# A fused cross-attention and squared-ReLU feed-forward on one core: loads, transposes and PSUM banks rearranged

## The chip, the core and the metric

The kernel runs on one core of a Trainium2 chip. A core has a matrix engine (TensorE, PE in the profile, with its weight loads as PEld), VectorE (DVE), ScalarE (ACT), GpSimd (POOL), SyncE (SP), which here only issues transfers, and 16 DMA engines that all queues share. The metric is device time in microseconds, smaller is better.

## What is computed

```python
# x: (B=8, H=8, S=512, D=64); state: (8, 8, Ns=32, 64)
scores = scale * x @ state.T              # per batch and head, softmax over the 32 slots
xread  = softmax(scores, -1) @ state      # 512 rows read the state
scores2 = scale * state @ x.T             # softmax over the 512 rows
sread  = softmax(scores2, -1) @ x         # 32 slots read x
a = concatenate([xread, sread], axis=2)   # (8, 8, 544, 64) -> 4352 rows of 512
h = a @ w_in                              # 512 -> 2048
g = s * relu(h)**2 + b
out = g @ w_out                           # 2048 -> 512, float32
```

## The kernel before, in words

Matrix operands are float16, sums float32. Heads are handled in two groups g of four; a group's four times 32 slots fill the 128 partitions. For each batch b:

- `att_stT` (L186) transposes the batch's state on TensorE; `att_xT` (L199), called twice, does so with x in eight 128x128 matmul transposes each, and DVE copies them out of PSUM.
- `att_T` (L216): scores T, 16 matmuls of 64x32 weights, into two one-bank tiles; ScalarE takes exponentials E (L235) with the row sums rs.
- `att_D` (L244), once per group: a matmul with a block matrix of ones sums E over the slots; logarithm L (L249), exponential R of its negative (L251), and a4 = E * R on DVE are the softmax weights.
- `att_M` (L256): the product of the state with w_in, M, in four chunks c of 512 columns, so that mm1 can multiply a4 straight with M (xread @ w_in without xread). Eight matmuls per chunk, into two one-bank tiles.
- `att_aT` (L278): E divided by its row sums on DVE (a2), eight TensorE transposes and a DVE copy make aT; `att_V` (L293) multiplies x (as weights) with 32 columns of aT, 32 matmuls, and writes the slot reads, already transposed, into srdT for all batches.
- `mm1_f` (L331), for each of 16 chunks f of 128 hidden columns: two matmuls of 512 columns into h, ReLU on ScalarE (r, L340; for a third of batch 0's chunks on DVE, L338), square on DVE (g, L342). In the trace h, r and g have f in their names.
- `mm2_part` (L347): the output tile o of 128 rows (rr, four per batch) sums 16 matmuls of 512 columns, in four parts of four (here called units); DVE scales and adds the bias (osb, L361), and SP stores it (L362).

TensorE's order is written out by hand. Of 16 slots per batch, each gives one mm1 chunk, then the pieces of the attention of the next batch (the lists in `pieces` and `first`), then one unit of mm2, which lags 20 slots behind mm1. After batch 7 come 16 slots of mm1 for the 256 slot reads (`mm1_sr`, h_sr), mixed with the last units, and two output tiles of slot reads. `bias` sums w_out with 16 matmuls and one more product in the mm2 of batch 0. `warm_up` issues matmuls on zeros before the first real ones. The tile framework orders the other engines by their priorities and adds the waits.

Loads: SP brings x of batch 0 as float32 in four pieces (xf, L92), which DVE and ScalarE cast (L116). Pool loads and casts in one DMA each: four chunks of w_in (wi, L144), x of batches 1 to 7 (xn, L134), four chunks of w_out (wo, L154), and twice the state of batches 2 to 7 (L169), side by side, as the transposes need it. The state of batches 0 and 1 comes as float32 (stf), and Pool casts batch 0's (L123).

PSUM has 8 banks: three buffers of one bank for the attention (psA), three for h (psH), two for o (psO).

Of the kernel before, what the change touches and what calls it, by code (L numbers as in the profile page):

```python
# [14 lines left out]
def kernel(  # L15
# [10 lines left out]

    nc = tc.nc
    AF = mybir.ActivationFunctionType  # L30
    ALU = mybir.AluOpType

# [7 lines left out]
    NG = H // 4  # L40
    NPAIR = H // 2
# [3 lines left out]
    NFC = DF // FC  # L45
    scale = float(1.0 / np.sqrt(D))
# [7 lines left out]
    mpool = ctx.enter_context(tc.tile_pool(name="mpool", bufs=2))  # L54
# [3 lines left out]
    psA = ctx.enter_context(tc.tile_pool(name="psA", bufs=3, space=bass.MemoryType.PSUM))  # L58
    psH = ctx.enter_context(tc.tile_pool(name="psH", bufs=3, space=bass.MemoryType.PSUM))
# [25 lines left out]
    st_v = state.rearrange("b (g hf) j d -> (hf j) (b g) d", g=NG)
    stf = konst.tile([P, 2 * NG, D], FP32, name="stf")
    xf = konst.tile([P, H, SCH * D], FP32, name="xf")
    x0_v = x[0].rearrange("h (q c) d -> q h (c d)", q=P)
    nc.scalar.dma_start(stf[:, 0:NG, :], st_v[:, 0:NG, :])
    nc.scalar.dma_start(ident16, ident_dr.ap())  # L90
    for i in range(4):
        nc.sync.dma_start(xf[:, 2 * i : 2 * i + 2], x0_v[:, 2 * i : 2 * i + 2])  # L92
    nc.scalar.preload_act_table_set("natural_log_exp_and_others")
# [12 lines left out]
    srdT = konst.tile([P, NPAIR, B * Ns], FP16, name="srdT")

    st16 = konst.tile([P, B * NG, 2, D], FP16, name="st16")
    xn = {}
    xn[0] = xpool.tile([P, H, SCH, D], FP16, name="xn_0")

    def cast_x0(eng, i):
        eng(  # L116
            xn[0][:, 2 * i : 2 * i + 2].rearrange("p h c d -> p h (c d)"),
            xf[:, 2 * i : 2 * i + 2],
        )

    def cast_st(eng, b):
        for k in range(2):
            eng.tensor_copy(st16[:, b * NG : b * NG + NG, k, :], stf[:, b * NG : b * NG + NG])  # L123

    cast_st(nc.gpsimd, 0)
    cast_x0(nc.vector.tensor_copy, 0)
    cast_x0(nc.scalar.copy, 1)
    cast_x0(nc.vector.tensor_copy, 2)
    cast_x0(nc.scalar.copy, 3)
    cast_st(nc.vector, 1)  # L130

    def load_x(b):
        xt = xpool.tile([P, H, SCH, D], FP16, name=f"xn_{b}")
        nc.gpsimd.dma_start(  # L134
            out=xt.rearrange("p h c d -> p h (c d)"),
            in_=x[b].rearrange("h (q c) d -> q h (c d)", q=P),
        )
        xn[b] = xt

    wi = []  # L140

    def load_wi(c):
        t = wpool.tile([P, NKM, FC], FP16, name=f"wi_{c}")
        nc.gpsimd.dma_start(  # L144
            out=t,
            in_=moe_w_in.rearrange("(k p) f -> p k f", p=P)[:, :, c * FC : (c + 1) * FC],
        )
# [12 lines left out]
    load_wi(0)  # L160
    load_wi(1)
    load_x(1)
    load_wi(2)
    load_wi(3)
    for q in range(4):
        load_wo(q)
    load_x(2)
    for k in range(2):
        nc.gpsimd.dma_start(out=st16[:, 2 * NG :, k, :], in_=st_v[:, 2 * NG :, :])  # L169
    for b in range(3, B):  # L170
        load_x(b)
# [4 lines left out]
    def head_of(g, q):  # L176
        return 4 * g + (q if g == 0 else q ^ 1)

    def chunk_of(cc):

        return 2 * (cc % 2) + cc // 2


    A = {}

    def att_stT(b):  # L186
        ps = att_ps([P, NG, P], FP16, f"stTps_{b}")
        for g in range(NG):
# [10 lines left out]
    def att_xT(b, i):  # L199
# [10 lines left out]
        if b == 0 and i == 1:  # L210
            nc.scalar.copy(xT, ps)
        else:
            nc.vector.tensor_copy(xT, ps)
# [291 lines left out]
```

## Time and profile before

| | us |
|---|---|
| median of the three runs (257.17 to 259.74) | 257.67 |
| span of the profiled execution, first to last instruction | 256.8 |
| TensorE busy | 235.6 |
| DVE busy | 146.6 |
| ScalarE busy | 118.1 |
| last matmul ends | 249.1 |

The profiled execution's own time is not listed apart from its span; the median lies 0.9 us above the span. Times in a timeline or a chain are counted from the span's start. A row of the timeline gives start, duration, engine, line, operation, output <- inputs, shapes, and in brackets how long the engine had been idle and what ended that.

### The profile page before, as it was taken

To read this page: it belongs to the slowest core of one execution; us is meant where nothing else is said; L and a number is where in the kernel's file an instruction comes from. 1 tells how busy PE (TensorE), PEld (TensorE's weight loads), DVE (VectorE), ACT (ScalarE), POOL (GpSimd) and SP (SyncE) were. 2 spreads that over 40 slices of the span, in tenths; PEclk is the share of its full clock that TensorE was granted. 3 is DMA by queue.
4 is the path that set the end of the run, shared out by engine and by line. 5 is a ranking of instruction groups with operands and counts; after the bars stand their busy time and mean duration, and the time that the engine had idled before them with its cause. 6 is when DMAs were issued, how large, how long until landed. Compare 5 with 4: busy or idle time off the path is not lost.

```text
span 256.8 us, 4444 instructions
## 1 busy us (share of the span) xinstructions
PE 235.6 (92%) x1772; PEld 108.9 (42%) x1772; DVE 146.6 (57%) x327; ACT 118.1 (46%) x255; POOL 15.0 (6%) x23
## 2 busy tenths in 40 slices
PE   8189759997999999999999999999999999999970
PEld 3034214442543454445434544454344444555430
DVE  1128968777468745874587458745874444433220
ACT  2074564862457445743574357435743444222000
POOL 6524210000000000000000000000000000000000
PEclk9679986999999999999999999999999999999998
DMA  7999999901111111111111111111101211121111
GB/s 169 198 195 207 203 181 198 139 0 41 43 41 41 43 41 43 41 41 46 41 43 41 43 41 44 40 41 43 52 31 46 79 42 41 43 82 41 50 52 65
DMA packets 21709, 18.71 MB, mean 73 GB/s; under 512 B 5048, under 2 KB 17336, under 8 KB 21688
## 3 DMA queue, kind: packets, MB, share of 16 engines
q0 software_dynamic: 14608, 8.26, 22.9%
q1 hardware_dynamic: 6664, 10.06, 11.3%
q8 instruction: 14, 0.23, 0.4%
q10 hardware_dynamic: 416, 0.10, 0.2%
q14 instruction: 7, 0.06, 0.1%
HBM read 17.76 MB, written 8.91 MB: 104 GB/s over the span
## 4 chain that ended last, share of the span: by engine, by line
PE 83%; DVE 6%; DMA 4%; ACT 2%; issue 1%; SPq 1%
DMA xf<-in_x_dram 4%; PE o_2_2011 L66 1%; PE o_3_974 L66 1%; PE o_2_2372 L66 1%; PE o_1_1921 L66 1%; PE o_2_2733 L66 1%; PE o_2_1650 L66 1%; PE o_2_1289 L66 1%; PE o_1_1199 L66 1%; PE o_0_728 L66 1%; PE o_1_2643 L66 1%; PE o_1_2282 L66 1%; PE o_1_1560 L66 1%; PE o_3_2109 L66 1%; PE o_3_1748 L66 1%; PE o_0_2554 L66 1%
## 5 line engine op out<-in xcount | busy, mean ns | idle before, releaser
L66 PE MATMUL warm_ps<-warm 128*128 128x512 f16 x26 | 9.9, 521 | 7.1 <-DVE stT_171 L196 5.2
L66 PEld LDWEIGHTS <-warm 128*128 128x128 f16 x26 | 3.0, 124 | 10.6 <-issue 9.0
L116 DVE CAST xn_115<-xf 128x512 f16<-128x512 f32 x2 | 0.9, 452 | 9.2 <-DMA xf<-in_x_dram 9.2
L116 ACT CAST xn_115<-xf 128x512 f16<-128x512 f32 x2 | 1.2, 618 | 9.5 <-DMA xf<-in_x_dram 9.5
L66 PEld LDWEIGHTS <-M_253 128*128 128x128 f16 x32 | 2.6, 103 | 6.0 <-DVE M_253 L276 3.5
L66 PEld LDWEIGHTS <-M_1502 128*128 128x128 f16 x32 | 3.1, 98 | 3.8
L66 PEld LDWEIGHTS <-M_760 128*128 128x128 f16 x32 | 3.1, 98 | 3.8
L66 PEld LDWEIGHTS <-M_1863 128*128 128x128 f16 x32 | 3.1, 98 | 3.8
L66 PEld LDWEIGHTS <-M_2224 128*128 128x128 f16 x32 | 3.1, 98 | 3.8
L66 PEld LDWEIGHTS <-M_2585 128*128 128x128 f16 x32 | 3.1, 98 | 3.8
L66 PEld LDWEIGHTS <-M_1141 128*128 128x128 f16 x32 | 3.1, 98 | 3.8
L66 PEld LDWEIGHTS <-M_493 128*128 128x128 f16 x32 | 2.9, 98 | 3.1 <-issue 0.2
L66 PEld LDWEIGHTS <-stT_171 64*32 64x32 f16 x48 | 1.1, 89 | 5.1 <-issue 4.9
L66 PEld LDWEIGHTS <-xn_115 128*64 128x64 f16 (+1 forms) x48 | 2.0, 115 | 1.8 <-issue 1.0
L340 ACT ACTIVATE r_11_898<-h_11_895 128x512 f16<-128x512 f32 x1 | 0.6, 597 | 4.5 <-PE h_11_895 L66 4.5
L66 PEld LDWEIGHTS <-st_114 128*128 128x128 f16 x16 | 1.6, 102 | 2.2 <-POOL st_114 L123 0.4
L66 PEld LDWEIGHTS <-bones_91 128*128 128x128 f16 x16 | 1.5, 98 | 2.1 <-issue 0.6
L66 PE MATMUL bias_ps<-wsum,ones_105 128*128 128x512 f32 x2 | 1.1, 644 | 1.4 <-DVE wsum L391 1.4
L361 DVE SCALAR_TENSOR_TENSOR osb_sr_3261<-o_sr_3244,s_bc,bias_bc 128x512 f32<-128x512 f32 x1 | 0.8, 751 | 2.7 <-PE o_sr_3244 L66 2.7
L361 DVE SCALAR_TENSOR_TENSOR osb_sr_3281<-o_sr_3264,s_bc,bias_bc 128x512 f32<-128x512 f32 x1 | 0.8, 751 | 2.7 <-PE o_sr_3264 L66 2.7
L361 DVE SCALAR_TENSOR_TENSOR osb_3_3241<-o_3_3224,s_bc,bias_bc 128x512 f32<-128x512 f32 x1 | 0.8, 750 | 2.7 <-PE o_3_3224 L66 2.7
L66 PEld LDWEIGHTS <-stT_312 64*32 64x32 f16 x48 | 0.7, 94 | 3.7 <-issue 3.7
(1753 smaller groups left out, 768.1 us busy)
## 6 DMA issues: line engine op xcount, KB each, us to landing
xf<-in_x_dram SPq DMA_DIRECT2D x4, 256.0 KB, 9.2
wi_124<-in_moe_w_in_dram POOLq DMA_DIRECT2D x1, 512.0 KB, 8.9
wi_126<-in_moe_w_in_dram POOLq DMA_DIRECT2D x1, 512.0 KB, 11.7
xn_128<-in_x_dram POOLq DMA_DIRECT2D x1, 512.0 KB, 12.4
wi_130<-in_moe_w_in_dram POOLq DMA_DIRECT2D x1, 512.0 KB, 14.0
wi_132<-in_moe_w_in_dram POOLq DMA_DIRECT2D x1, 512.0 KB, 15.8
wo_134<-in_moe_w_out_dram POOLq DMA_DIRECT2D x1, 512.0 KB, 17.7
wo_136<-in_moe_w_out_dram POOLq DMA_DIRECT2D x1, 512.0 KB, 20.5
```

Source lines behind the costliest of these rows:

```text
L66: return nc.tensor.matmul(out, lhsT, rhs, start=start, stop=stop, tile_position=tp, is_transpose=is_transpose, skip_group_check=True,)
L116: eng(xn[0][:, 2 * i : 2 * i + 2].rearrange("p h c d -> p h (c d)"), xf[:, 2 * i : 2 * i + 2],)
L340: nc.scalar.activation(r16, hps, AF.Relu)
L361: nc.vector.scalar_tensor_tensor(osb, ops, s_bc, bias_bc, ALU.mult, ALU.add)
```

## The change

- Heads are grouped otherwise: group g has the heads 2q + g, so that a group's heads share a half of the partitions.
- Loads: x of batch 0 comes in two pieces of 512 KB, one per group. TensorE, SP and Pool now run in the written order. Pool first casts the state of batch 0, which waits for its load, and then issues w_in; x of batch 1 stands after the third chunk of w_in instead of the second. The state of batches 2 to 7 is loaded once and then doubled by a Pool copy. The block matrix of ones is made by memsets instead of a load.
- PSUM: psA has two buffers of two banks, psH two buffers. Scores of both groups go into one two-bank tile (one exponential per group), D of both groups and M of both groups too, evacuated by one instruction of 1024 columns on DVE or ScalarE ("dve", "act") or half on each ("split"). In batch 0 every second h takes an o buffer.
- Batches 0 and 1 still transpose x on TensorE; from batch 2 on SP issues a DMA transpose. E is transposed by DMA for all batches (ET), undivided; `att_aT` is gone.
- `att_V` takes ET as weights, 32 columns wide, and x as the moving operand, 64 columns, on four column tiles; the 128x64 result per group is divided by the row sums afterwards (sr), and `att_srT` transposes it on TensorE into srdT.
- Order: all 16 chunks of batch 0's mm1 go first, with M of batches 0 and 1 between them, three units of mm2, then slots as before. V comes in slots 12 to 15. The last output tile is made in two halves of 256 columns.
- Stores go to Pool's queue, those of slot reads as four of 32 rows each; only the two last halves go to SP.

The rows below are the instructions in each engine's order, without times. First Pool's queue from its first kernel instruction on (wi, wo, xn and st as above). Before:

```order
L144 DMA wi_124<-in_moe_w_in_dram 128x4x512
L144 DMA wi_126<-in_moe_w_in_dram 128x4x512
L123 CAST st_114<-stf 128x2x64 x2
L134 DMA xn_128<-in_x_dram 128x8x256
L144 DMA wi_130<-in_moe_w_in_dram 128x4x512
```

And now:

```order
L421 CAST st_91<-stf 128x2x64 x2
L110 DMA wi_98<-in_moe_w_in_dram 128x4x512
L110 DMA wi_99<-in_moe_w_in_dram 128x4x512
L110 DMA wi_100<-in_moe_w_in_dram 128x4x512
L421 CAST st_91<-stf 128x2x64 x2
L104 DMA xn_107<-in_x_dram 128x8x256
L110 DMA wi_101<-in_moe_w_in_dram 128x4x512
```

The cast of batch 0's state, which waits for a load, went ahead of all weights. Further on in the same queue, the state of batches 2 to 7, before and now:

```order
L134 DMA xn_142<-in_x_dram 128x8x256
L169 DMA st_114<-in_state_dram 128x12x64 x2
L134 DMA xn_146<-in_x_dram 128x8x256
L134 DMA xn_148<-in_x_dram 128x8x256
L134 DMA xn_150<-in_x_dram 128x8x256
```

```order
L104 DMA xn_108<-in_x_dram 128x8x256
L435 DMA st_91<-in_state_dram 128x12x64
L436 COPY st_91<-st_91 128x12x64
L104 DMA xn_109<-in_x_dram 128x8x256
L104 DMA xn_110<-in_x_dram 128x8x256
```

The second load of the state became a copy that Pool runs itself, ahead of x of batch 3. SP's queue, where after the first loads only stores stood, now reads from its fourth transfer on (ET: transposed E, xT: transposed x of the next batch but one):

```order
L432 DMA s_bc<-in_moe_s_dram 128x1
L433 DMA b_bc<-in_moe_b_dram 128x1
L241 DMA_TRANSPOSE ET_254<-E_210 128x8x128
L241 DMA_TRANSPOSE ET_507<-E_463 128x8x128
L169 DMA_TRANSPOSE xT_511<-xn_108 128x16x128
L241 DMA_TRANSPOSE ET_639<-E_610 128x8x128
L169 DMA_TRANSPOSE xT_643<-xn_109 128x16x128
```

From batch 2 on a pair of transposes per batch goes through this one queue, in order. The diff, cut to its core:

```diff
-    psA = ctx.enter_context(tc.tile_pool(name="psA", bufs=3, space=bass.MemoryType.PSUM))
-    psH = ctx.enter_context(tc.tile_pool(name="psH", bufs=3, space=bass.MemoryType.PSUM))
+    psA = ctx.enter_context(tc.tile_pool(name="psA", bufs=2, space=bass.MemoryType.PSUM))
+    psH = ctx.enter_context(tc.tile_pool(name="psH", bufs=2, space=bass.MemoryType.PSUM))
...
+    def head_of(g, q):
+        return NG * q + g
+
...
+    def att_xT_dma(b):
+        xT = new_xT(b)
+        nc.sync.dma_start_transpose(
+            out=xT.rearrange("p h k t -> p (h k) t"),
+            in_=xn[b].rearrange("p h c d -> p (h c d)"),
+        )
...
+        T = att_ps([P, 2, 512], FP32, f"T_{b}_{gs[0]}")
...
+            nc.scalar.activation(
+                a["E"][:, g, :].rearrange("p (m t) -> p m t", m=2),
+                T[:, :, 256 * i : 256 * i + 256],
+                AF.Exp,
+                scale=scale,
+                accum_out=a["rs"][:, g : g + 1],
+            )
...
+        nc.scalar.activation(a["L"][:, sl], Dps, AF.Ln)
+        nc.scalar.activation(a["R"][:, sl], a["L"][:, sl], AF.Exp, scale=-1.0)
+        nc.vector.tensor_mul(a["a4"][:, sl], a["E"][:, sl], a["R"][:, sl])
...
+        ps = att_ps([P, NG, FC], FP32, f"Mps_{b}_{c}")
...
+        if how == "split":
+            nc.vector.tensor_copy(dst[:, 0], ps[:, 0])
+            nc.scalar.copy(dst[:, 1], ps[:, 1])
+        elif how == "act":
+            nc.scalar.copy(dst, ps)
+        else:
+            nc.vector.tensor_copy(dst, ps)
...
+    def att_ET(b):
+        a["ET"] = apool.tile([P, NG * SCH, P], FP16, name=f"ET_{b}", tag="ET")
+        nc.sync.dma_start_transpose(out=a["ET"], in_=a["E"].rearrange("p g t -> p (g t)"))
+        a["rq"] = apool.tile([P, NG], FP32, name=f"rq_{b}", tag="rq")
+        nc.vector.reciprocal(a["rq"], a["rs"])
...
+        ps = att_ps([P, NG, D], FP32, f"V_{b}")
+            for c in range(SCH):
+                for q in range(NQ):
+                    mm(
+                        ps[32 * q : 32 * q + 32, g, :],
+                        a["ET"][:, SCH * g + c, 32 * q : 32 * q + 32],
+                        xn[b][:, head_of(g, q), chunk_of(c), :],
+                        start=(c == 0),
+                        stop=(c == SCH - 1),
+                        tp=(0, 32 * q),
+                    )
+        a["sr"] = apool.tile([P, NG, D], FP16, name=f"sr_{b}", tag="sr")
+        for g in range(NG):
+            nc.vector.tensor_scalar(a["sr"][:, g], ps[:, g], a["rq"][:, g : g + 1], None, ALU.mult)
+
+    def att_srT(b):
+        ps = att_ps([P, NQ, Ns], FP16, f"srT_{b}")
+        mm(
+            ps.rearrange("p q j -> p (q j)"),
+            A[b]["sr"].rearrange("p g d -> p (g d)"),
+            ident16,
+            is_transpose=True,
+        )
...
+    def evac(ops, key, rr, n0, n1, dmas):
+        osb = opool.tile([P, n1 - n0], FP32, name=f"osb_{key}_{rr}_{n0}", tag="osb")
+        nc.vector.scalar_tensor_tensor(osb, ops, s_bc, bias_bc[:, n0:n1], ALU.mult, ALU.add)
+        for eng, p0, p1, dst in dmas:
+            eng.dma_start(dst, osb[p0:p1])
...
+    def dmas_of(key, rr, eng):
+        if key != "sr":
+            return [(eng, 0, P, x_dst(key, rr))]
+        return [
+            (eng, Ns * i, Ns * i + Ns, out_BSn[4 * rr + i, S:ST, :]) for i in range(4)
+        ]
...
+    def mm2_halves(key, rr):
+        for n0 in (0, DM // 2):
+            n1 = n0 + DM // 2
+            ops = psO.tile([P, DM // 2], FP32, tag="o", name=f"o_{key}_{rr}_{n0}")
+            for f in range(NKF):
+                mm(
+                    ops,
+                    G[key, f][:, P * rr : P * rr + P],
+                    wof(f)[:, n0:n1],
+                    start=(f == 0),
+                    stop=(f == NKF - 1),
+                )
+            evac(ops, key, rr, n0, n1, [(nc.sync, 0, P, x_dst(key, rr)[:, n0:n1])])
...
+    with tc.manual_schedule(engines={ET.PE, ET.SP, ET.Pool}):
+        nc.vector.memset(warm, 0.0)
+        for g in range(NG):
+            nc.sync.dma_start(
+                xf[:, g],
+                x[0, g :: NG].rearrange("h (q c) d -> q h (c d)", q=P),
+            )
+        nc.scalar.dma_start(stf[:, 0:2, :], st_v[:, 0:2, :])
+        nc.scalar.dma_start(ident16, ident_dr.ap())
+        nc.scalar.preload_act_table_set("natural_log_exp_and_others")
+        nc.sync.dma_start(stf[:, 2:4, :], st_v[:, 2:4, :])
+        nc.vector.memset(bones16, 0.0)
+        for q in range(4):
+            nc.vector.memset(bones16[32 * q : 32 * q + 32, 32 * q : 32 * q + 32], 1.0)
+        nc.vector.memset(ones16, 1.0)
+        nc.vector.memset(ones32, 1.0 / Ns)
+
+        def cast_st(eng, b0, b1):
+            for k in range(2):
+                eng.tensor_copy(st16[:, 2 * b0 : 2 * b1, k, :], stf[:, 2 * b0 : 2 * b1])
+
+        cast_st(nc.gpsimd, 0, 1)
+        for c in range(2):
+            load_wi(c)
+        load_wi(2)
+        cast_st(nc.gpsimd, 1, 2)
+        load_x(1)
+        load_wi(3)
+        for q in range(4):
+            load_wo(q)
+        nc.sync.dma_start(s_bc, moe_s.to_broadcast((P, 1)))
+        nc.sync.dma_start(b_bc, moe_b.to_broadcast((P, 1)))
+        load_x(2)
+        nc.gpsimd.dma_start(out=st16[:, 4:, 0, :], in_=st_v[:, 4:, :])
+        nc.gpsimd.tensor_copy(st16[:, 4:, 1, :], st16[:, 4:, 0, :])
+        for b in range(3, B):
+            load_x(b)
...
+        b0 = {
+            0: [],
+            1: [lambda: att_M(0, 1, "split")],
+            2: [lambda: att_M(1, 0, "split")],
+            5: [lambda: att_M(0, 2, "split")],
+            6: [lambda: att_M(1, 1, "split")],
+            8: [lambda: att_xT_pe(1, 0)],
+            9: [lambda: att_M(0, 3, "split")],
+            10: [lambda: att_xT_pe(1, 1)],
+            11: [lambda: att_M(1, 2, "dve")],
+            12: [lambda: att_T(1, [0, 1])],
+            14: [lambda: att_M(1, 3, "act")],
+            15: [lambda: att_D(1, [0, 1])],
         }
-        LAG = 20
-        for slot in range(NKF * (B + 1)):
-            s, f = divmod(slot, NKF)
-            if s < B:
-                mm1_x(s, f, dve_relu=(s == 0 and f % 3 == 1))
-            else:
-                mm1_sr(f)
-            if s == 0:
-                todo = first.get(f, [])
-            else:
-                todo = [fn for at, fn in pieces(s + 1) if at == f] if s + 1 < B else []
-            for fn in todo:
+        for f in range(NKF):
+            mm1_x(0, f)
+            for fn in b0.get(f, []):
                 fn()
-            if slot >= LAG:
-                mm2_slot(slot - LAG)
-        for u in range(NKF * (B + 1) - LAG, NKF * B):
-            mm2_slot(u)
-        for rr in range(B * Ns // P):
-            mm2_part("sr", rr, 0, NKF, sr_dst(rr))
+        att_ET(1)
+        att_xT_dma(2)
+        for i in range(3):
+            unit(units[i])
+        todo = units[3:]
+
+        def pieces(s):
+            nb = s + 1
+            out = {}
+
+            def at(f, fn):
+                out.setdefault(f, []).append(fn)
+
+            if nb < B:
+                at(0, lambda: att_stT(nb))
+                at(3, lambda: att_T(nb, [0, 1]))
+                at(3, lambda: att_M(nb, 0, "dve"))
+                at(4, lambda: att_ET(nb))
+                if nb + 1 < B:
+                    at(4, lambda: att_xT_dma(nb + 1))
+                at(5, lambda: att_D(nb, [0, 1]))
+                at(7, lambda: att_M(nb, 1, "dve"))
+                at(7, lambda: att_M(nb, 2, "act"))
+                at(10, lambda: att_M(nb, 3, "act"))
+            if s == 1:
+                at(12, lambda: att_V(0))
+                at(13, lambda: att_srT(0))
+            at(14, lambda: att_V(s))
+            at(15, lambda: att_srT(s))
+            return out
+
+        for s in range(1, B):
+            todo_s = pieces(s)
+            for f in range(NKF):
+                mm1_x(s, f)
+                for fn in todo_s.get(f, []):
+                    fn()
+                if s == 1 and f == 2:
+                    bias()
+                unit(todo.pop(0))
+        for f in range(NKF):
+            mm1_sr(f)
+            if todo:
+                unit(todo.pop(0))
+        for u in todo + sr_units:
+            unit(u)
+        mm2_halves(last_b, SCH - 1)
```

More of the change, by code (lines that the diff above doesn't have):

```diff
@@ L85 @@
[L85 to L93, printed above, removed]
@@ L121, in cast_st @@
[L121 to L130, printed above, removed]
+    srdT = konst.tile([P, NKM, B * Ns], FP16, name="srdT")
+    st_v = state.rearrange("b (n hf) j d -> (hf j) (b n) d", n=2)
+    wi = [wpool.tile([P, NKM, FC], FP16, name=f"wi_{c}") for c in range(NFC)]
@@ L162 @@
[L162 to L171, printed above, removed]
     def wof(f):
         return wo[f // 4][:, f % 4, :]
[L176 to L184, printed above, removed]
+    A = {b: {} for b in range(B)}
     def att_stT(b):
-        ps = att_ps([P, NG, P], FP16, f"stTps_{b}")
-        for g in range(NG):
-            mm(
-                ps[:, g, :],
-                st16[:, b * NG + g].rearrange("p k d -> p (k d)"),
+        ps = att_ps([P, 2, P], FP16, f"stTps_{b}")
+        for n in range(2):
+            mm(
+                ps[:, n, :],
+                st16[:, 2 * b + n].rearrange("p k d -> p (k d)"),
@@ L208, in att_xT, with att_T @@
                 )
[L209 to L216 removed]
+        xT = A[b]["xT"] if g else new_xT(b)
+        dst = xT.rearrange("p (q g) k t -> p g q k t", g=NG)[:, g]
+        if b == 0:
+            h2 = NQ // 2
+            nc.vector.tensor_copy(dst[:, 0:h2], ps[:, 0:h2])
+            nc.scalar.copy(dst[:, h2:NQ], ps[:, h2:NQ])
+        else:
+            nc.vector.tensor_copy(dst, ps)
[5 more added lines that the diff above has]
+        )
+    def att_T(b, gs):
         a = A[b]
[L219 to L221 removed]
+        n = len(gs)
+        T = att_ps([P, 2, 512], FP32, f"T_{b}_{gs[0]}")
+        for q in range(NQ):
+            for i, g in enumerate(gs):
                 h = head_of(g, q)
@@ L423 @@
-    with tc.manual_schedule(engines={mybir.EngineType.PE}):
-        warm_up(9)
+    units = []
+    for b in range(B):
+        for i in range(NKF):
+            rr, part = divmod(i, 4)
+            if b == 0:
+                rr, part = 2 * (i // 8) + i % 2, i % 8 // 2
+            units.append((b, rr, part))
+    sr_units = [("sr", rr, part) for rr in range(B * Ns // P) for part in range(4)]
+    last_b = B - 1
+    tail = [u for u in units if u[0] == last_b and u[1] == SCH - 1]
+    units = [u for u in units if u not in tail]
```

306 lines of the change are left out of this document (109 added, 197 removed).

## The prediction, made before the changed kernel was run

> **What bounds the kernel now.** I read the page first: its busy row and the slices of PE, its clock and the DMA engines.
>
> ```profile
> span 256.8 us, 4444 instructions
> PE 235.6 (92%) x1772; PEld 108.9 (42%) x1772; DVE 146.6 (57%) x327; ACT 118.1 (46%) x255; POOL 15.0 (6%) x23
> PE   8189759997999999999999999999999999999970
> PEclk9679986999999999999999999999999999999998
> DMA  7999999901111111111111111111101211121111
> ```
>
> A slice is 6.4 us. TensorE is full from the eighth slice on; before that it has holes and a lower granted clock, and just there the DMA engines are nine tenths busy. So there are two regimes: loads and the first batch's dependencies up to about 50 us, then TensorE. The second view cuts the span at events: first mm1 product (21.87), first mm1 of batch 1 (43.62), first mm1 of the state rows (217.80), last matmul (249.13). Its columns after the stretch's length are PE, PEld, DVE, ACT and POOL busy, PE clock, DMA share and GB/s.
>
> ```profile
> 0.00:21.87 21.87, 14.07 (x87) 5.86 (x87) 6.46 (x19) 7.79 (x17) 10.62 (x18) 0.84 1.09 190
> 21.87:43.62 21.75, 17.40 (x190) 6.85 (x188) 18.00 (x41) 11.44 (x26) 4.37 (x5) 0.84 1.48 196
> 43.62:217.80 174.18, 172.82 (x1327) 79.02 (x1323) 111.09 (x244) 92.71 (x197) 0.00 (x0) 1.00 0.16 47
> 217.80:249.13 31.33, 31.33 (x177) 17.13 (x175) 10.25 (x24) 6.14 (x16) 0.00 (x0) 1.00 0.15 52
> 249.13:256.80 7.67, 0.00 (x0) 0.00 (x0) 0.75 (x1) 0.00 (x0) 0.00 (x0) 0.84 0.20 65
> ```
>
> From 43.62 to 249.13 us TensorE idles 1.4 us: there only removed TensorE work counts. The first 43.6 us and the last 7.7 us are latency.
>
> **Start: x of batch 0 ahead of the weights.** The timeline shows when its four pieces are cast, which is when they landed, and when Pool issued the first weight load and cast the state.
>
> ```profile
> 1.24 0.89 POOL L144 DMA_DIRECT2D wi_124<-in_moe_w_in_dram  x1 [0.79 <-POOLq L489]
> 3.82 0.43 DVE L116 CAST xn_115<-xf 128x512 f16<-128x512 f32 x1 [2.50 <-DMA xf<-in_x_dram]
> 4.04 0.58 POOL L123 CAST st_114<-stf 128x128 f16<-128x128 f32 x2 [1.18 <-DMA stf<-in_state_dram]
> 4.90 0.62 ACT L116 CAST xn_115<-xf 128x512 f16<-128x512 f32 x1 [1.83 <-DMA xf<-in_x_dram]
> 10.95 0.48 DVE L116 CAST xn_115<-xf 128x512 f16<-128x512 f32 x1 [6.71 <-DMA xf<-in_x_dram]
> 13.19 0.62 ACT L116 CAST xn_115<-xf 128x512 f16<-128x512 f32 x1 [7.68 <-DMA xf<-in_x_dram]
> 17.70 0.60 ACT L249 ACTIVATE L_0_239<-D_0_237 128x512 f32<-128x512 f32 x1
> 18.77 0.62 ACT L251 ACTIVATE R_0_241<-L_0_239 128x512 f16<-128x512 f32 x1
> 21.87 0.38 PE L66 MATMUL h_0_302<-a_0_0_243,M_253 128*128 128x512 f16 x1
> ```
>
> Two pieces landed 1.08 us apart, the next two, beside the weights, 6 and 2.2 us later. In the change Pool casts the state first, so the weights start at about 4.6 instead of 1.24, and the pieces should follow at 1.08 us: the last at about 7.1 instead of 13.19. From that cast to the first mm1 lie 8.7 us here. In the change ScalarE's chain behind it is two exponentials, an xT half, two logarithms and two reciprocal exponentials, seven operations of 0.6 us like the L and R shown; with the cast, transposes, scores and M's copy around them I estimate 7.4 us. The first mm1 then comes at 14.5, 7.4 us earlier.
>
> What follows is batch 0's mm1 with M of batches 0 and 1. DVE was busy 18.0 of 21.75 us; it loses batch 1's aT copy and a2 scalings and some M copies. So the stage takes no more than 21.75; with 21 TensorE reaches the state transposes of batch 2 at 36, against 44.22. But these wait for a load:
>
> ```profile
> 14.06 0.89 POOL L134 DMA_DIRECT2D xn_142<-in_x_dram  x1 [2.85 <-DMA wi_126<-in_moe_w_in_dram]
> 19.74 1.01 POOL L169 DMA_DIRECT2D st_114<-in_state_dram  x1 [1.49 <-DMA wi_130<-in_moe_w_in_dram]
> 22.28 0.87 POOL L134 DMA_DIRECT2D xn_146<-in_x_dram  x1 [1.54 <-DMA wi_132<-in_moe_w_in_dram]
> xn_142<-in_x_dram POOLq DMA_DIRECT2D x1, 512.0 KB, 21.9
> xn_146<-in_x_dram POOLq DMA_DIRECT2D x1, 512.0 KB, 18.9
> ```
>
> x of batch 2 (xn_142) landed at 14.06 + 21.9 = 36.0 and x of batch 3 at 22.28 + 18.9 = 41.2; between them came the state twice and 512 KB. Weights landed 2.5 us apart (wi_130 and wi_132, for which Pool waited until 19.74 and 22.28), so each state load took some 1.3 us. The change has the same loads up to x of batch 2; weights start later but x of batch 0 is out of their way, so I keep 36.0. One state load makes 37.3, and then Pool, not a second DMA, doubles it: six times the elements of the 0.29 us cast above, up to 1.7 us. The state is ready at 39.0. So of 8.2 us gained on the engines, the load leaves 44.2 - 39.0 = **5.2 us**; bounds 8.2 (loads come sooner) and 0.
>
> **TensorE work.** The chain of waits runs through TensorE back to back there, so its pieces are prices:
>
> ```profile
> 43.07 0.61 PE V_607 L66 x32
> 44.22 0.11 PE stTps_648 L66 x2
> 44.33 0.45 PE xTps_0_653 L66 x8
> 47.53 0.86 PE o_0_728 L66 x4
> 59.75 1.13 PE bias_ps L66 x2
> 109.83 0.45 PE aTps_1572 L66 x8
> ```
>
> xT (two groups of eight) leaves TensorE for batches 2 to 7: 6 x 0.90 = 5.4 us. aT leaves for all, six of them behind 44.2: 6 x 0.45 = 2.7. Three mm2 units of batch 0 now run before batch 2's state transposes, where none had: 3 x 0.86 = 2.6. Against that, V of batches 0 and 1 moves behind: 1.2, and eight single transposes of sr come in: 8 x 0.06 = 0.5. V keeps 32 matmuls but streams 64 columns in 32-wide tiles, four side by side instead of two. No row has this shape; I take the same 0.61, since 19 ns per matmul is nearer to issue than to streaming; bounds half and double, -2.4 to +4.9 over eight. T, D and M keep count and size. Scores and M now take two PSUM banks per instruction: fewer, longer ACT and DVE operations, hidden, as ACT is busy 92.71 of 174.18 us. Net: 5.4 + 2.7 + 2.6 - 1.2 - 0.5 = **9.0 us**.
>
> **DMA transposes.** They cost nothing if each batch's pair (xT 512 KB, ET 256 KB) lands within a batch, 25.58 us now and 25.58 - 0.90 - 0.45 + 0.06 = 24.3 after, counted from its first mm1:
>
> ```profile
> 94.95 0.43 PE h_0_1364 L66 x2
> 120.53 0.43 PE h_0_1725 L66 x2
> q10 hardware_dynamic: 416, 0.10, 0.2%
> q1 hardware_dynamic: 6664, 10.06, 11.3%
> ```
>
> The trace holds no such transfer. The nearest rows are queues: ScalarE's q10 moved 240-byte packets, 0.2% of 16 x 256.8 us over 416, about 20 ns each; q1's 1.5 KB packets took 70 ns. As 256-byte rows a pair is 3072 packets, 192 per engine, 3.8 us; as 32-byte pieces 1536 per engine, 30.3 us. I take the first, because both q10's loads have 256-byte rows as the 128-column blocks here do: xT 2.6 us and a landing of some 2 us. The first xT, of batch 2, can start at 36.0; its scores come after three units (2.6), three mm1 (1.3) and the bias sum (1.13 for its last product, as much for the first sums and the DVE copy between: 3.4) behind 39.0, at 46.3. Hidden, with 10 us of room. SP has nothing else to do by then: the stores went to Pool, whose later issues nobody waits for within four output buffers. The Trainium skill, DMA: Bandwidth & Descriptors, section Latency and other measured facts, has 261 GB/s for a DMA transpose; by that estimate a pair takes 3.0 us and the sum stays. No run here shows it yet.
>
> **End.** The last rows and SP's waits:
>
> ```profile
> 248.75 0.38 PE L66 MATMUL o_sr_3264<-wo_140,g_sr_3215 128*128 128x512 f16 x1
> 249.16 0.75 DVE L361 SCALAR_TENSOR_TENSOR osb_sr_3281<-o_sr_3264,s_bc,bias_bc 128x512 f32<-128x512 f32 x1 [2.70 <-PE o_sr_3264 L66]
> 249.94 0.59 SPq L362 DMA_DIRECT2D out_dram<-osb_sr_3281  x1
> SPq L500 <- DMA out_dram<-osb_sr_3281: 3.1, 1, 3.1
> SPq L500 <- DMA out_dram<-osb_sr_3261: 1.4, 1, 1.4
> out_dram<-osb_3_3241 SPq DMA_DIRECT2D x1, 256.0 KB, 2.0
> ```
>
> SP stops issuing at 250.53, waits 1.4 + 3.1 and reaches 255.1, leaving 1.7 to the end. The last store writes four blocks and is slow; a plain 256 KB store lands in 2.0. In the change the last are halves on SP: 0.4 (half a DVE operation) + 2.0 + 1.7 = 4.2 us. Pool's state stores may end later: its last evacuation ends 2.7 us before the last matmul, four issues at up to 0.89 us and 2.0 to land give 2.9 + 1.7 = 4.6. Gain 7.7 - 4.6 = **3.1 us** (bounds 0 and 3.5).
>
> **Sum.** 256.8 - 5.2 - 9.0 - 3.1 = 239.5 us of span; the runs' median 257.67 is 0.9 above the span, so 240.4.
>
> **Rivals.** (1) *The loads take the start back.* If ET transposes and the late weights push the state of batch 2 to 44.2, the 5.2 us are gone and TensorE, idle, restarts slow: both early stages show a mean clock of 0.84, 16% missing of 21.75 us, 3.5 us lost. With 2 of them: 247.6. For it: DMA nine tenths busy to 50 us. Against: same bytes, x out of the way. The Trainium skill, TensorE: Matmul & The Clock Gate, Part 1, says that an idle window of about 3.4 us halves the clock; the trace agrees with its 0.84, and a wait from 36 to 39 would just escape it.
>
> (2) *The transposes become the bound.* At 30.3 us a pair, SP's queue, not TensorE, sets the batch: scores of batch 2 come at 36 + 20.2 + 2 = 58.2 instead of 46.3, and five more batches take 30.3 instead of 24.3 us: 12 + 30 = 42 us later, 282 us. It decides the sign from a pair price of 26 us (0.67 x 26 + 38 - 46.3 + 5 x 1.7 = 17.5, the whole gain). For it: packets below 512 bytes are slow per byte here, q10 against q1. Against: it needs the smallest pieces. The Trainium skill, DMA: Bandwidth & Descriptors, section Specifications, puts line rate at 512 B and more, which speaks against this change; q10's 12 GB/s per engine against q1's 22 agree.
>
> (3) *The loads come sooner*: x of batch 2 at 33, the engines set 36, and V runs at half price: 240.4 - 3 - 2.4 = 235.0.
>
> **How the numbers follow.** Forecast 0.70 (its own range 235 to 246: load 36 to 43, V to double), rival 1 0.14, rival 2 0.10, rival 3 0.06. Within 1% (about what a measurement of this kernel tells from no change) is 255.1 to 260.2: a tenth of rival 2 and 0.02 of rival 1, 0.03; slower the rest of rival 2, 0.09; faster 0.88. The range runs from 233, below rival 3, to 252, rival 1 with V at double price; it leaves out rival 2 and the forecast's edges.
>
> **What would show it.** Right: last cast of x of batch 0 near 7, first mm1 near 14.5, the state transposes of batch 2 near 39 behind Pool's copy, a batch of 24.3 us with a full TensorE, the pair of transposes under 10 us, 4 to 5 us after the last matmul. Wrong: TensorE waiting for xT each batch, or a start no earlier than 21 us.

## The result, and the profile after

The changed kernel takes 241.36 us in the median of four runs (240.68 to 242.45), the kernel before 258.60 beside it (four runs, 257.17 to 259.74): ratio 0.933, 95% interval 0.928 to 0.938. The forecast was 240.4. Its three gains came in other sizes than forecast: 2.4 us at the start instead of 5.2, 11.3 in TensorE's stretch instead of 9.0, 4.2 at the end instead of 3.1.

The page of the changed kernel, its span, busy row and slices (now 6 us each):

```profile
span 238.9 us, 4115 instructions
PE 219.0 (92%) x1631; PEld 97.7 (41%) x1631; DVE 120.4 (50%) x268; ACT 123.0 (51%) x213; POOL 36.0 (15%) x64
PE   6787860989999999999999999999999999999994
PEclk9999997699999999999999999999999999999999
DMA  7999999999094711171117112511211112111113
```

The hole in the seventh slice (36 to 42 us) lies where the DMA engines are still full, and the clock is down in the two slices from it on. Behind it TensorE is at 80% or more in every slice but the last. The same cut at events as before: first mm1 product (14.50), state transposes of batch 2 (41.78), last matmul (235.41).

```profile
14.50:41.78 27.28, 16.41 (x139) 5.78 (x137) 15.32 (x32) 13.69 (x24) 2.39 (x4) 0.95 1.31 176
...
235.41:238.90 3.49, 0.00 (x0) 0.00 (x0) 0.48 (x1) 0.00 (x0) 0.00 (x0) 1.00 0.28 96
```

In the stretch from 14.50 to 41.78 TensorE works 16.4 of 27.3 us: the first mm1 comes 7.4 us earlier than before, and most of that is lost again here. The timeline shows to what:

```profile
14.50 1.03 PE L64 MATMUL h<-a,M 128*128 128x512 f16 x4
39.76 1.65 SPq L169 DMA_TRANSPOSE xT<-xn  x1
40.89 0.83 POOL L436 COPY st<-st 128x768 f16<-128x768 f16 x1 [22.25 <-DMA st<-in_state_dram]
41.66 4.37 POOL L104 DMA_DIRECT2D xn<-in_x_dram  x5
41.78 0.39 PE L64 MATMUL stTps<-ident,st 128*128 128x128 f16 x2 [6.92 <-POOL st L436]
50.88 0.43 PE L64 MATMUL T<-xT,stT 64*32 64x256 f16 x16
```

TensorE was ready at 34.86 (41.78 - 6.92) and waited for the state, which landed at 40.8. x of batch 2, for which SP waited, came at 39.6. Both are some 3.5 us later than the prediction's 36.0 and 37.3. Pool stood behind the state load all that time and issued x of batches 3 to 7 only at 41.66; this turns out to matter. The last row is the start of batch 2's scores, the mark that I follow through the experiments.

The chain of waits gives one batch's attention pieces, back to back on TensorE (start, duration):

```profile
78.30 0.43 PE D L64 x2
78.73 0.86 PE o L64 x4
...
81.33 0.56 PE Mps L64 x16
81.88 0.97 PE o L64 x4
...
85.87 0.34 PE Mps L64 x8
...
91.50 0.35 PE V L64 x32
...
98.59 0.36 PE T L64 x16
98.95 0.22 PE Mps L64 x8
...
101.87 0.43 PE D L64 x2
```

From D to D a batch takes 23.57 us, 25.58 before. V costs 0.35 us instead of 0.61. Eight M products cost 0.34 alone, but 0.22 right behind another piece, and 16 in a row 0.56. The mm2 unit that follows such a piece takes 0.97 us instead of 0.86.

### The profile page after: what moved, and what is told of

Its sections match the earlier page's. It is cut to its first block, busy times and chain, and to the rows that moved or that the text cites. A ratio compares the mean times of both kernels' runs of the same rounds, so it can differ in the third digit from the quotient of the medians.

```text
span 238.9 us, 4115 instructions
## 1 busy us (share of the span) xinstructions
PE 219.0 (92%) x1631; PEld 97.7 (41%) x1631; DVE 120.4 (50%) x268; ACT 123.0 (51%) x213; POOL 36.0 (15%) x64
## 4 chain that ended last, share of the span: by engine, by line
PE 80%; DMA 16%; POOL 1%; DVE 1%; issue 0%; ACT 0%
PE o L64 47%; PE h L64 20%; DMA st<-in_state_dram 10%; DMA wi<-in_moe_w_in_dram 4%; PE h_sr L64 3%; PE o_sr L64 3%; PE Mps L64 3%; DMA stf<-in_state_dram 2%; PE V L64 1%; PE D L64 1%; PE T L64 1%; POOL wi L110 1%; PE bias_ps L64 0%; PE stTps L64 0%; POOL st L436 0%
## 5 line engine op out<-in xcount | busy, mean ns | idle before, releaser
L64 PE MATMUL o<-wo,g 128*128 128x512 f16 (+1 forms) x528 | 132.8, 377 | 0.1
L287 ACT ACTIVATE r<-h 128x512 f16<-128x512 f32 x123 | 73.0, 596 | 83.8 <-PE h L64 83.8
L289 DVE TENSOR_TENSOR g<-r 128x512 f16<-128x512 f16 x128 | 53.7, 423 | 62.0 <-ACT r L287 61.9
L64 PE MATMUL h<-a,M 128*128 128x512 f16 x256 | 76.6, 382 | 1.8 <-DVE a L214 0.8
L64 PEld LDWEIGHTS <-g 128*128 128x128 f16 x528 | 49.3, 98 | 55.5 <-issue 8.4
L320 POOL DMA_DIRECT2D out_dram<-osb x31 | 16.8, 543 | 160.1 <-DVE osb L318 152.9
L64 PEld LDWEIGHTS <-M 128*128 128x128 f16 x256 | 24.3, 98 | 33.0 <-issue 4.0
L318 DVE SCALAR_TENSOR_TENSOR osb<-o,s_bc,bias_bc 128x512 f32<-128x512 f32 (+1 forms) x33 | 24.1, 729 | 2.7 <-PE o L64 2.7
L236 DVE CAST M<-Mps 128x1024 f16<-128x1024 f32 x13 | 15.8, 1217 | 0.0
L234 ACT CAST M<-Mps 128x1024 f16<-128x1024 f32 x13 | 13.1, 1011 | 0.0
```

The lines of the kernel that those rows point to most:

```text
L64: return nc.tensor.matmul(out, lhsT, rhs, start=start, stop=stop, tile_position=tp, is_transpose=is_transpose, skip_group_check=True,)
L234: nc.scalar.copy(dst, ps)
L236: nc.vector.tensor_copy(dst, ps)
L287: nc.scalar.activation(r16, hps, AF.Relu)
L289: nc.vector.tensor_mul(gt, r16, r16)
L318: nc.vector.scalar_tensor_tensor(osb, ops, s_bc, bias_bc[:, n0:n1], ALU.mult, ALU.add)
```

## The experiments

Each is the changed kernel with one edit, timed beside the kernel before. None leaves out any work. The table gives, from each profile, where batch 2's scores start, the span, and the difference; then the median and the ratio to before.

| run | scores of b2 | span | rest | median | ratio (95%) |
|---|---|---|---|---|---|
| the change | 50.88 | 238.9 | 188.0 | 241.36 | 0.933 (0.928-0.938) |
| e1 x on TensorE | 52.48 | 245.2 | 192.7 | 246.19 | 0.949 (0.943-0.954) |
| e2 state early | 54.42 | 244.4 | 190.0 | 247.13 | 0.953 (0.947-0.959) |
| e4 weights first | 50.28 | 238.2 | 187.9 | 241.11 | 0.930 (0.922-0.937) |
| e5 ET late | 46.87 | 234.9 | 188.0 | 236.49 | 0.912 (0.906-0.917) |
| e6 old end | 51.89 | 244.1 | 192.2 | 245.55 | 0.951 (0.943-0.960) |
| e7 transposes twice | 51.11 | 239.4 | 188.3 | 242.06 | 0.939 (0.931-0.947) |
| e8 pieces apart | 52.42 | 243.0 | 190.6 | 243.87 | 0.943 (0.933-0.953) |
| e9 kept busy | 48.76 | 237.1 | 188.3 | 238.86 | 0.927 (0.919-0.935) |
| e10 state early, x held | 44.51 | 234.0 | 189.5 | 237.61 | 0.921 (0.915-0.928) |
| e11 ET late, kept busy | 45.61 | 234.3 | 188.7 | 234.88 | 0.912 (0.906-0.917) |
| e12 state early, x held, ET late | 41.90 | 229.8 | 187.9 | 233.02 | 0.904 (0.899-0.910) |
| e13 state by two loads | 53.77 | 242.5 | 188.7 | 246.19 | 0.954 (0.948-0.960) |

The column to look at is "rest": wherever the edit is about the start (e4, e5, e7, e9 to e13) it stays at 188 to 189.5 us, so that the first 55 us decide the difference within 1.5 us. Only e1, e6 and e8, which touch later work, change it by more, and e2 by 2 us (behind its long wait its clock is 0.61 from 55 to 60 us).

### The end (e6)

```diff
-        return [
-            (eng, Ns * i, Ns * i + Ns, out_BSn[4 * rr + i, S:ST, :]) for i in range(4)
-        ]
+        return [(nc.sync, 0, P, out_BSn[4 * rr : 4 * rr + 4, S:ST, :])]
...
-        for u in todo + sr_units:
+        for u in todo + tail + sr_units:
             unit(u)
-        mm2_halves(last_b, SCH - 1)
```

> The end as before the change: the last output tile of x in one piece and ahead of the slot reads, whose two tiles are stored by one transfer of four blocks each on SP. Theory: the time from the last matmul to the end goes back from 3.5 to 7.7 us, so about 245.5 us. Rival (the store's form does not matter, only the shorter last piece): 1 us longer, 242.4.

245.55 us. The rest is 4.2 us longer: the end's whole measured gain. Which share belongs to the order, to the halves and to the form of the store is not separated. On e6's timeline the last store, of a whole tile of four blocks, is issued 6.9 us before the end:

```profile
237.18 0.58 SPq L320 DMA_DIRECT2D out_dram<-osb_sr  x1
```

In the changed kernel the last matmul is followed by half an output tile, whose small store leaves 3.49 us to the end:

```profile
232.98 1.96 POOL L320 DMA_DIRECT2D out_dram<-osb_sr  x4 [1.47 <-DVE osb_sr L318]
...
235.43 0.48 DVE L318 SCALAR_TENSOR_TENSOR osb<-o,s_bc,bias_bc 128x256 f32<-128x256 f32 x1 [1.26 <-PE o L64]
```

### TensorE's work and the DMA transposes (e1, e7, e8)

e1 gives x back to TensorE for all batches:

```diff
-        att_xT_dma(2)
...
                 at(0, lambda: att_stT(nb))
+                at(0, lambda: att_xT_pe(nb, 0))
+                at(1, lambda: att_xT_pe(nb, 1))
...
-                if nb + 1 < B:
-                    at(4, lambda: att_xT_dma(nb + 1))
```

> x is transposed by TensorE for all batches; the DMA transposes of E stay. Theory (TensorE is full behind the state transposes of batch 2, DMA transposes are hidden): six batches take back 2 x 0.45 us each, 5.4 us, so about 246.8 us and a batch of 24.5 instead of 23.6 us. Rival (the DMA transposes of x cost something elsewhere, by contention with loads or by a wait): less than 4 us come back, under 245.4.

The ratio rises by 0.015, some 4 us. The starts of D in two successive batches on e1's timeline:

```profile
105.09 0.59 PE L64 MATMUL D<-E,bones 128*128 128x512 f16 x2
129.54 0.59 PE L64 MATMUL D<-E,bones 128*128 128x512 f16 x2
```

24.45 us a batch, 0.9 more than 23.57: the price that the prediction took from the old rows (2 x 0.45), and five batches of it make nearly all of the 4.7 us of "rest". So the cost on TensorE is fully paid when it is put there, and DMA took it over for nothing. e7 asks how much room DMA had left, by issuing each transpose from batch 2 on a second time into a spare tile (one more `dma_start_transpose` for xT and ET).

> Each DMA transpose from batch 2 on is issued a second time into a spare tile (E and x; nobody reads the copies). Theory (a pair takes some 7.5 us of SP's queue in a batch of 23.6 us and is hidden): the doubled pair takes 15 us, still hidden, 241 to 242 us. Rival (transposes slow stores, loads or TensorE's reads): more than 1% longer, over 244.

242.06 us, ratio unchanged within its interval. In e7's list of issues the transposes of x land about as before (number of issues, then the median us from issue to landing):

```profile
xT<-xn SPq DMA_TRANSPOSE x12, 4.2
```

and in the changed kernel:

```profile
ET<-E SPq DMA_TRANSPOSE x8, 2.8
xT<-xn SPq DMA_TRANSPOSE x6, 4.7
```

Issued twice, a pair is still far from the 24 us of a batch. e8 spreads the M chunks, which the change puts behind T and behind each other:

```diff
-                at(3, lambda: att_M(nb, 0, "dve"))
+                at(6, lambda: att_M(nb, 0, "dve"))
...
-                at(7, lambda: att_M(nb, 1, "dve"))
-                at(7, lambda: att_M(nb, 2, "act"))
-                at(10, lambda: att_M(nb, 3, "act"))
+                at(8, lambda: att_M(nb, 1, "dve"))
+                at(10, lambda: att_M(nb, 2, "act"))
+                at(12, lambda: att_M(nb, 3, "act"))
```

> The four chunks of M of each batch from 2 on stand in slots of their own (6, 8, 10, 12) instead of one behind the scores and two together. Theory (pieces of narrow tiles back to back save TensorE's refill between them): 0.1 us for the chunk behind the scores and 0.2 to 0.3 us for the pair, six times, 2 to 2.5 us longer, 243.5. Rival (the saving came from the two-bank tiles or the new head order and not from the place): 241.

243.87 us, a ratio 0.010 higher, some 2.6 us; the two intervals overlap, so the rows have to decide. D to D on e8's timeline:

```profile
103.84 0.59 PE L64 MATMUL D<-E,bones 128*128 128x512 f16 x2
127.87 0.59 PE L64 MATMUL D<-E,bones 128*128 128x512 f16 x2
```

24.03 us a batch, 0.46 more for the same matmuls: a 64x32 piece between full-size products costs more when it stands alone. Half of it lies in the pieces (four of 0.34 against 0.56, 0.34 and 0.22), half in two more mm2 units of 0.97 instead of 0.86. Over five to six batches this is the 2.6 us by which the rest grew.

### What the state of batch 2 waits for (e4, e5)

Two suspects make the loads late: the weights now start at 5.24 instead of 1.24, behind the state cast, and ET of batches 0 and 1 is transposed while they run. e4 issues two chunks of w_in ahead of the cast:

```diff
-        cast_st(nc.gpsimd, 0, 1)
         for c in range(2):
             load_wi(c)
+        cast_st(nc.gpsimd, 0, 1)
```

> Undoes the first part alone: Pool issues the first two chunks of w_in before it casts the state of batch 0, so x of batch 0 shares the DMA engines with weights. Theory (loads in total set the early stage): the first mm1 comes near 20 instead of 14.5 us, but the state of batch 2 lands no later than 40.8, perhaps 2 us sooner: 239 to 242 us. Rival (batch 0's chain sets the time one to one): 5 us longer, 246 to 247.

No difference (241.11), and on e4's timeline the state is no sooner. Nor is x of batch 0 later: its last cast starts at 6.81, with two chunks of weights issued ahead of it, and at 6.71 in the changed kernel. The expected 20 us for the first mm1 did not come (16.54; TensorE's transposes were slow in this execution, see the last section). In e4:

```profile
6.81 0.62 ACT L446 CAST xn<-xf 128x512 f16<-128x512 f32 x1 [1.00 <-DMA xf<-in_x_dram]
41.86 0.40 PE L64 MATMUL stTps<-ident,st 128*128 128x128 f16 x2 [6.29 <-POOL st L436]
```

and in the changed kernel:

```profile
6.71 0.62 ACT L446 CAST xn<-xf 128x512 f16<-128x512 f32 x1 [1.08 <-DMA xf<-in_x_dram]
```

e5 moves the two ET transposes behind the x transpose of batch 2 in SP's queue:

```diff
-        att_ET(0)
...
+        att_xT_dma(2)
+        att_ET(0)
         att_ET(1)
-        att_xT_dma(2)
```

> The DMA transposes of E of batches 0 and 1 are issued behind the first transpose of x instead of at 11 and 30 us, amid the loads. Theory (they take DMA time from the loads): x and state of batch 2 land 1.5 to 2.5 us sooner, 239 to 240 us. Rival (loads are slower than before for another reason): loads land as now, 241.

236.49 us: better than either theory allowed. In e5's timeline the loads land some 4.5 us sooner:

```profile
35.20 1.69 SPq L169 DMA_TRANSPOSE xT<-xn  x1
36.41 0.83 POOL L436 COPY st<-st 128x768 f16<-128x768 f16 x1 [18.73 <-DMA st<-in_state_dram]
37.29 0.39 PE L64 MATMUL stTps<-ident,st 128*128 128x128 f16 x2 [3.65 <-POOL st L436]
```

These are the prediction's 36.0 and 37.3 within a microsecond: its load times were right for a kernel without the ET transposes. The stretch in which ET of batch 0 is under way in the changed kernel (11.5 us from issue to landing, 2.8 in the median), first in the changed kernel, then in e5:

```profile
11.40:22.90 11.50, 8.91 (x68) 2.53 (x68) 8.67 (x19) 8.21 (x15) 3.23 (x4) 1.00 1.32 168
```

```profile
11.40:22.90 11.50, 9.67 (x77) 3.07 (x76) 9.01 (x20) 8.22 (x16) 3.34 (x4) 1.00 1.28 199
```

The DMA engines are as busy, but move 168 instead of 199 GB/s, with the transpose's own 256 KB among the 168. Over 11.5 us these are 0.36 MB less and 0.26 MB of other data: 0.62 MB of loads, 3.1 us at 199 GB/s. So the transpose displaced loads of more than twice its size.

### What stands beside the x transpose (e2, e10, e13)

e2 brings the state load ahead of w_out, to end TensorE's wait for it:

```diff
         load_wi(3)
+        nc.gpsimd.dma_start(out=st16[:, 4:, 0, :], in_=st_v[:, 4:, :])
         for q in range(4):
             load_wo(q)
...
         load_x(2)
-        nc.gpsimd.dma_start(out=st16[:, 4:, 0, :], in_=st_v[:, 4:, :])
         nc.gpsimd.tensor_copy(st16[:, 4:, 1, :], st16[:, 4:, 0, :])
```

> The one load of the state of batches 2 to 7 is issued ahead of w_out instead of behind x of batch 2; nothing else changes. Theory (the load of the state, not the engines, sets when TensorE goes on in batch 1): the state transposes of batch 2 start near 35.4 instead of 41.8 us; the next wait is for x of batch 2, which still lands near 40, so its scores start near 44.5 instead of 50.9: 235 to 236.5 us. Rival (the chain of batch 0 or the amount of TensorE work sets the time, the wait for the state is absorbed later): 241, unchanged.

I was wrong: 247.13, slower by 2% than the change. The state is early and TensorE transposes it at 36.15, without waiting, but another wait takes its place. In e2:

```profile
27.16 3.50 POOL L104 DMA_DIRECT2D xn<-in_x_dram  x4
36.15 0.27 PE L64 MATMUL stTps<-ident,st 128*128 128x128 f16 x2
40.85 5.34 SPq L169 DMA_TRANSPOSE xT<-xn  x1
54.42 0.65 PE L64 MATMUL T<-xT,stT 64*32 64x256 f16 x16 [11.22 <-DMA xT<-xn]
```

With the state early Pool gets past its copy and issues x of batches 3 to 7 from 27.16 instead of 41.66 on. x of batch 2 lands about as in the changed kernel (40.7 against 39.6), but its transpose now runs beside 2.5 MB of loads. The time from its issue to its landing, in e2 and in the changed kernel:

```profile
xT<-xn SPq DMA_TRANSPOSE x1, 13.5
```

```profile
xT<-xn SPq DMA_TRANSPOSE x1, 3.7
```

The expectations of e10, e12 and e13 have 8.1 us for the changed kernel. That is a misreading: 8.1 is the longest of its six x transposes, that of batch 3, issued at 66.64 beside stores. How the transpose and the loads share the DMA engines is seen in e2 from 46 to 53 us (q0 has Pool's loads, q1 SP's transpose; packets, MB, and their time as a share of 16 engines):

```profile
q0 software_dynamic: 1685, 0.85, 87.7%
q1 hardware_dynamic: 1686, 0.43, 46.4%
```

They take as many packets each, one for one, although those of the loads are twice as large. The Trainium skill, DMA: Bandwidth & Descriptors, section Queues, rings and completion order, says that a DMA engine with work in several queues takes turns between them, packet by packet. The trace agrees with its 1685 and 1686. A packet of the transpose comes every 66 ns on each engine (16 x 7 us over 1686), so that its 128 packets per engine take 8.5 us by this estimate. Alone they take under 2 us, by the rate of 291 GB/s that e10 shows from 42.2 to 43.8 us:

```profile
DMA packets 1816, 0.46 MB, mean 291 GB/s; under 512 B 1816, under 2 KB 1816, under 8 KB 1816
```

The rest falls mostly on the start: the issue on SP takes 5.34 us here and 1.65 in the changed kernel.

If this is the cause, the early state must pay once the loads are held back. e10 adds to e2 a Pool copy of one block of the transposed x ahead of them:

```diff
-        for b in range(3, B):
-            load_x(b)
...
         att_xT_dma(2)
+        hold = konst.tile([P, P], FP16, name="hold")
+        nc.gpsimd.tensor_copy(hold, A[2]["xT"][:, H - 1, 1, :])
+        for b in range(3, B):
+            load_x(b)
```

> The state load goes ahead of w_out as in the run with the state early (247.1 us), and x of batches 3 to 7 is loaded only once the transposed x of batch 2 has landed (a Pool copy of one block of it stands ahead of the loads). Theory: that run was slower because with the state early Pool no longer stood still before the loads of x 3 to 7, so that these ran beside the transpose of x 2, which landed 13.5 us after its issue instead of 8.1. Held back, the transpose lands some 5 us after x of batch 2 (40.9), the scores of batch 2 start near 46 instead of 50.9 in the changed kernel: 236 to 238.5 us. Rival: the early state itself, or w_out behind it, cost the time: 246 to 248 us as there.

237.61 us, a ratio of 0.921 against e2's 0.953. In e10:

```profile
40.84 1.64 SPq L169 DMA_TRANSPOSE xT<-xn  x1
44.51 0.43 PE L64 MATMUL T<-xT,stT 64*32 64x256 f16 x16 [1.31 <-DMA xT<-xn]
```

The transpose is issued at the same time, lands after 3.6 us instead of 13.5, and the scores start 9.9 us sooner. And the other way round: if the changed kernel owes something to Pool's standing still, it must get slower without. e13 undoes the one part of the change that makes Pool wait:

```diff
-        nc.gpsimd.tensor_copy(st16[:, 4:, 1, :], st16[:, 4:, 0, :])
+        nc.gpsimd.dma_start(out=st16[:, 4:, 1, :], in_=st_v[:, 4:, :])
```

> One part of the change undone: the state of batches 2 to 7 is loaded twice, as in the kernel before, instead of once with a copy on Pool; so nothing holds Pool before the loads of x 3 to 7. Theory: these then run beside the transpose of x of batch 2, which lands 13 us or more after its issue instead of 8.1, and the scores of batch 2 start near 54.5 instead of 50.9: 244 to 246 us. Rival: what stands beside the transpose does not matter, and the copy and the second load cost the same within 0.5 us: 240.5 to 242 us.

246.19 us, ratio 0.954: some 5 us lost by the ratio (3.6 between the two profiled executions). In e13, with the x loads of batches 3 on issued from 25.20 on:

```profile
39.40 5.62 SPq L169 DMA_TRANSPOSE xT<-xn  x1
53.77 0.44 PE L64 MATMUL T<-xT,stT 64*32 64x256 f16 x16 [2.80 <-DMA xT<-xn]
```

The landing took 14.3 us here, against 3.7 in the changed kernel. There the Pool copy, which replaced a load, protects the transpose by holding up the queue behind it.

### The clock after the wait (e9, e11)

e9 lets TensorE multiply zeros while it waits for the state; e11 does the same in e5, with 15 products:

```diff
+                if s == 1 and f == 0:
+                    warm_up(28)
                 for fn in todo_s.get(f, []):
                     fn()
```

> 28 matmuls on zeros stand ahead of the state transposes of batch 2, where TensorE idles 6.9 us and then runs at a granted clock of 0.59 for 5 us. Theory (the idle time lowers the clock): the matmuls behind the wait run at 0.216 us each at once, 2 to 2.5 us shorter, 239. Rival (the slow matmuls come from loads or from operands that are late): unchanged, 241.

> The ET transposes of batches 0 and 1 behind the x transpose of batch 2 (236.5 us alone), and 15 products of zeros (3.3 us) in TensorE's wait for the state, which was 3.65 us there with a clock of 0.57 and 0.75 in the ten us behind it. Theory: the idle time lowers the clock even in a wait this short, about 2 us are lost: 234 to 235 us. Rival: the low clock is not from the idle time, or the wait is too short to matter: 236 to 237 us.

e9: 238.86 us, with an interval that overlaps the changed kernel's, so the rows have to decide. The five us behind the wait, in the changed kernel and in e9 (the clock is third from the end):

```profile
42.00:47.00 5.00, 5.00 (x22) 1.78 (x24) 1.05 (x3) 0.80 (x2) 4.03 (x5) 0.59 1.05 146
```

```profile
42.00:47.00 5.00, 4.20 (x31) 1.66 (x29) 1.77 (x4) 1.19 (x2) 4.01 (x5) 1.00 1.20 176
```

The same work from state transposes to scores takes 9.1 us (41.78 to 50.88) with the clock at 0.59 and 7.0 (41.76 to 48.76) with it at 1.00: 2.1 us. e11's clock is 1.00 throughout, and the same work takes 7.0 us instead of 9.6 in e5. But its products of zeros outlast the wait: the state transposes start at 38.62, 1.3 us later than in e5, so that the scores start only 1.3 us sooner. Its ratio (0.912) is e5's: behind a wait of 3.65 us the effect on the whole is not settled. In e5 the clock was 0.57 from 35 to 40 us, in the middle of which its wait ends, and 0.75 in the five us after. In e10 TensorE idled twice between 40 and 45 us, for 0.80 and 1.31 us, and it stayed at 1.00. The Trainium skill, TensorE: Matmul & The Clock Gate, Part 1, lets the clock halve after an idle window of about 3.4 us. The waits of 6.92 and 3.65 us, with a low clock, and the two short ones, without, agree.

### Together (e12)

State early, x of batches 3 to 7 held, and both ET transposes behind the x transpose: the edits of e10 and e5.

> State early, x 3 to 7 held back until x 2 is transposed, and the ET transposes of batches 0 and 1 behind that. Theory: nothing runs beside the loads up to x 2 and nothing beside its transpose; TensorE need not wait for the state (engines ready at 33.6), x 2 lands near 36.4, its transpose near 41, the scores of batch 2 start near 41 to 42 instead of 46.9: 230 to 233 us. Rival: the transpose takes 8 us with or without loads beside it, or the order of TensorE's work allows no earlier start: 234 to 237 us.

233.02 us, at the upper edge of what was expected, ratio 0.904 (0.899 to 0.910): the fastest version here. It is clear of the changed kernel's interval; those of e5 and e11 it overlaps. In e12:

```profile
34.91 0.27 PE L64 MATMUL stTps<-ident,st 128*128 128x128 f16 x2
36.37 1.69 SPq L169 DMA_TRANSPOSE xT<-xn  x1
40.19 0.29 POOL L485 COPY hold<-xT 128x128 f16<-128x128 f16 x1 [15.80 <-DMA xT<-xn]
41.90 0.43 PE L64 MATMUL T<-xT,stT 64*32 64x256 f16 x16
```

Between the state transposes and the scores TensorE waits for no load, and the x transpose lands 1.7 us ahead of them.

## Why the prediction was right, and which terms were not

- **What bounds the kernel.** Held: TensorE's work counts one for one behind the state transposes of batch 2 (e1, e8), and doubling the DMA transposes there changes nothing (e7).
- **First mm1 at 14.5.** 14.50 in the profiled execution, TensorE ready for the state transposes at 34.86 (36 forecast). The last cast of x of batch 0 came at 6.71 (7.1 forecast), but not for the reason given, that the weights are out of its way: with two chunks of weights ahead it comes at 6.81 (e4). What brings it sooner stays open; x now comes in two pieces, issued by 1.7 us, where the kernel before took four, issued by 2.7. Not all executions start so: e1, e4, e6 to e9, e11 and e12 have it at 15.9 to 16.5. In the changed kernel it decides nothing, since the loads are later.
- **The start, 5.2 us: measured 2.4.** The step that failed is "the change has the same loads up to x of batch 2 ... so I keep 36.0". It left out what the change adds to the DMA engines in that very stage, 512 KB through the ET transposes of batches 0 and 1. e5 shows the cost: 4.5 us of load time. That the weights start behind the cast costs nothing (e4). Pool's copy took 0.83 us, not 1.7.
- **Rival 1, in part.** It named the ET transposes and the clock. The state came at 41.8, not 44.2, but TensorE waited 6.92 us; "from 36 to 39 would just escape" failed with the load times, and the low clock cost 2.1 us (e9), 3.5 forecast there. Rival 3 had x of batch 2 at 33; it came at 39.6.
- **TensorE's work, 9.0 us: measured 11.3**, although the clock's 2.1 us are lost inside it; so the work fell by 13.4. Mis-sized were two: V takes 0.35 us, not the "same 0.61", 2.1 us over eight batches, at the lower bound's side; and pieces that stand next to each other cost less, 0.46 us a batch (e8), which no term had. The batch confirms it: 24.3 forecast, less 0.26 and 0.46 is 23.58; 23.57 measured. The xT term (0.90 a batch) was right (0.88 in e1). V's new form, the dropped aT and the two-bank tiles were not undone one by one; their shares are read from rows.
- **The DMA transposes cost nothing.** Right from batch 3 on, with room for twice as many (e7). The x transpose lands in 4.7 us in the median (2.6 + 2 forecast). A pair is 3072 packets of 256 bytes, 2.7 us at the 291 GB/s that e10 shows (3.8 forecast). The Trainium skill, DMA: Bandwidth & Descriptors, section Latency and other measured facts, has 261 GB/s for a DMA transpose, which would make 3.0 us, as an estimate. The trace is near it. So rival 2, which asked for 30.3 us a pair, is out. For batch 2 the transpose was issued 3.8 us late, landed after 3.7 us, and the scores started 7.5 us later. That it landed so soon is owed to Pool's wait, which I had not seen: without it the landing took 14.3 us, and the scores waited for it (e13).
- **The end, 3.1 us: measured 4.2**, just beyond its bound of 3.5. Pool's state stores, which I feared as the last, were issued 0.5 us before the last matmul ended and did not hold up the end.
- **The sum.** The errors of the start (+2.8) and of the other two (-3.4) nearly cancel: 238.9 us of span, 239.5 forecast. Part of the agreement is therefore luck. What lies around the span was 1.8 us in the profiled execution (240.68), 0.9 forecast.

## What to carry to other kernels

A transpose that moved from the matrix engine to DMA was free here where the DMA engines idle, but in a stage that waits for loads it must be counted among the loads, at more than its bytes, and the loads at it: put it behind the load that is waited for, and hold the next loads back until it has landed. When a wait is taken away, look at what it held up: here a Pool copy, waiting for its data, kept 2.5 MB of loads off a transpose, and the kernel got slower each time that wait was taken away alone (e2, e13). Price small matmul pieces with their neighbours, since the same eight products cost 0.34 us alone and 0.22 behind another piece.

## What the runs showed of the hardware

- A DMA transpose of 512 KB between on-chip tiles landed in 3.6 to 3.8 us with little beside it (the changed kernel, e10, e12), in 13.5 and 14.3 us beside 2.5 MB of loads (e2, e13); its issue on SP, 1.65 us, took 5.3 to 5.6 us there.
- Beside loads of another queue the transpose got one packet for each of theirs (1686 and 1685 in 7 us of e2).
- Alone a transpose moved 291 GB/s (e10), the loads without one 199 (e5), both together 168 (the changed kernel); the busy share of the DMA engines was about the same, 1.28 to 1.32.
- In the thirteen traces of the changed kernel and its variants the first eight x transposes on TensorE took 0.61 us in five and 1.06 in eight, with the same TensorE instructions ahead of them, the row of the granted clock at 1.00 in both. Why is not settled; it moves the first mm1 by 1.4 to 2 us.
